# A decode step on one core: the down weights' second load in three parts, the residual on TensorE, one store

## The chip, the core and the metric

The kernel runs on one core of a Trainium2 chip. The core has a matrix engine (TensorE, PE in the profile), three engines for elementwise work (VectorE or DVE, ScalarE or ACT, GpSimd or POOL), an engine that mostly issues transfers (SyncE or SP), and 16 DMA engines that move data between the chip's memory (HBM) and the on-chip memory SBUF. TensorE writes its results to PSUM, a small accumulator memory of 8 banks. The metric is the device time of one execution in microseconds, the median over runs.

## The reference

One decode step of a transformer block: attention over a cache, then a gated feed-forward layer, each behind a layer norm and with a residual. There are 4 sequences (B), one new token each, 512 features (D), 32 heads of 128, a cache of 8192 keys and values per head, and 1792 hidden features (F). All tensors are bf16.

```python
def _A_ref(x, k_cache, v_cache, wq, wo):
    q = (x @ wq).reshape(B, Sq, H, Dh) ...            # per head
    scores = einsum("bhqd,bhkd->bhqk", q, k_cache) * Dh ** -0.5
    o = einsum("bhqk,bhkd->bhqd", softmax(scores), v_cache)
    return o.reshape(B, Sq, H * Dh) @ wo

def _B_ref(x, w_gate, w_up, w_down):
    return (sigmoid(x @ w_gate) * (x @ w_up)) @ w_down

h = x + _A_ref(layernorm(x), k_cache, v_cache, wq, wo)
h2 = h + _B_ref(layernorm(h), w_gate, w_up, w_down)   # the result, 4 x 1 x 512
```

The two caches are 268 MB each, so nearly all of the 551 MB that the kernel reads is cache.

## The kernel before

The program is written out by hand for each engine: `emit` appends an instruction to one engine's list, with tokens of the work it waits for, `prog.dma` does the same for a transfer, and `play` writes the lists out. A token is a semaphore and a value; the 16 DMA engines raise a transfer's semaphore, so one transfer counts 16. Each engine executes its list in order.

**The streaming part.** The 128 pairs of sequence and head are handled as 32 units of 4. For each unit SP loads the keys (8 MB, `k`) and the values (8 MB, `v`) into one of three slots of the SBUF tensor `KV`. VectorE transposes the keys (L334), TensorE computes the scores (L343), ScalarE the exponentials (L368), and TensorE the products with the values (L404). SP's queue holds, in this order: wq, the caches unit by unit, then `wo`, `w_gate`, `w_up` and the down weights. A load is issued when its slot is free; the DMA engines work through the queue in order.

**The tail.** After the last unit's products TensorE projects with `wo` (L474, L479), which leaves h in PSUM (`h_ps`). `layernorm` (L272 to L286) normalises it and writes it transposed. ScalarE copies h to SBUF as `h_sb` in two halves of 256 columns (L485, partitions 0 to 3 and 32 to 35). TensorE computes gate and up (`glu`, L493), ScalarE the sigmoid (L504), VectorE the product and its transposes (L510, L513). The result `hhT` has 14 tiles of 128 hidden features. `down(t)` (L518) multiplies tile t with the down weights: two matmuls, one for each half of the 512 output columns, in different columns of the array, so that the halves lie at PSUM partitions 0 to 3 and 32 to 35 of bank `DN`. VectorE adds `h_sb` (L526) into `o_sb`, SP and ScalarE store a half each (L556), and SP waits for both stores (L558).

**The down weights.** `WDT = (0, 8, 12, 14)` cuts the 14 tiles into three loads, of tiles 0 to 7 (1024 KB), 8 to 11 (512 KB) and 12 and 13 (256 KB), each over all 128 partitions (L554). A tile's matmul waits for its load's token `t_wd`. The second load has one row of 4096 B per partition.

**Filler.** `filler(n)` (L387) issues matmuls whose result nobody reads, in stretches where TensorE waits. Four of them stand ahead of the first `down`.

## Time and profile before

| | |
|---|---|
| median of three runs | 1279.16 us (1279.07 to 1279.24) |
| the profiled execution | 1279.28 us, its span 1278.0 us |
| PE, DVE, ACT busy | 61%, 60%, 5% of the span |
| HBM read | 550.77 MB, 431 GB/s over the span |
| mean granted TensorE clock | 0.814 of full speed |
| the second down load | 512 KB, 32.9 us from issue to landing |

The span runs from the first to the last event of one profiled execution on the core; the execution's own time has 1.28 us more around it. In the profile L518 is line 518 of the kernel before, `KV<-in_B_w_down_dram` a transfer from the down weights into `KV`, SPq and ACTq the issuing of transfers by SP and ScalarE. In a stretch, the DMA share is the busy share of the 16 DMA engines, so a share of 0.06 is one engine at work. The chain of waits is followed back from the last instruction: each piece is what released the next. PEld is TensorE's loading of weights into its array.

### The profile page before, as it was taken

Reading aid. Unit: us, or ns where it says so; the run is one execution under the profiler, and the core shown is the slowest. Engines: PE = TensorE matmul, PEld = TensorE weight load, DVE = VectorE, ACT = ScalarE, POOL = GpSimd, SP = SyncE. Lnnn points to the kernel's source line nnn. Section 1 sums busy time; section 2 is a strip of 40 time slices with the busy share of each in tenths; the row PEclk is TensorE's granted clock in tenths of the full one; section 3 lists DMA queues with packets and bytes.
Section 4 is the critical chain, followed back from the end, with each engine's and each line's share of the span. In section 5 each row is a group of like instructions: output and inputs, shape, how many; then the busy total and the mean of one; then the engine's idle time right before and its main releaser. Section 6 shows DMA issues by size and latency. Waiting matters only on the chain.

```text
span 1278.0 us, 14081 instructions
## 1 busy us (share of the span) xinstructions
PE 782.9 (61%) x4590; PEld 328.4 (26%) x4641; DVE 762.3 (60%) x917; ACT 58.7 (5%) x114; POOL 5.7 (0%) x22
## 2 busy tenths in 40 slices
PE   1676765557755557655567655567555576555577
PEld 0232222223222223222222222222222232222233
DVE  1876665556665557665567655566655566655571
ACT  2000000000000000000000000000000000000001
POOL 1000000000000000000000000000000000000000
PEclk8788877788877788777788777888777888777889
DMA  9999999999999999999999999999999999999998
GB/s 425 429 425 429 427 449 435 427 429 429 453 429 427 429 435 447 429 429 427 445 437 429 429 427 449 433 429 429 427 449 435 427 429 431 449 431 427 429 437 360
DMA packets 10252, 550.83 MB, mean 431 GB/s; under 512 B 1148, under 2 KB 1160, under 8 KB 1416
## 3 DMA queue, kind: packets, MB, share of 16 engines
q1 hardware_dynamic: 10232, 550.77, 99.7%
q8 instruction: 2, 0.03, 0.0%
q14 instruction: 2, 0.02, 0.0%
q10 hardware_dynamic: 16, 0.01, 0.0%
HBM read 550.77 MB, written 0.00 MB: 431 GB/s over the span
## 4 chain that ended last, share of the span: by engine, by line
DMA 60%; PE 20%; DVE 12%; issue 2%; ACT 1%; SPq 0%; DVEq 0%
DMA KV<-in_A_k_cache_dram 58%; PE PS L343 15%; DVE kT L334 12%; PE PS L404 5%; DMA KV<-in_B_w_down_dram 3%; ACT kT L409 1%; PE PS L414 0%; SPq L538 0%; DVE PTz L374 0%; PE PS L518 0%; DVE KV L526 0%; SPq L554 0%; DVEq L112 0%
## 5 line engine op out<-in xcount | busy, mean ns | idle before, releaser
L343 PE MATMUL PS<-kT,Lq 128*128 128x512 bf16 x2048 | 592.0, 422 | 342.6 <-DVE kT L334 325.5
L334 DVE STREAM_TRANSPOSE kT<-KV 128x1024 f32<-128x1024 f32 x512 | 614.2, 1231 | 302.7 <-DMA KV<-in_A_k_cache_dram 237.9
L343 PEld LDWEIGHTS PS<-kT,Lq 128*128 x2048 | 211.0, 103 | 696.4 <-issue 624.2
L374 DVE STREAM_TRANSPOSE PTz<-E_sb 32x512 bf16<-32x512 bf16 x128 | 89.9, 703 | 128.9 <-PE PS L414 125.2
L404 PE MATMUL PS<-KV,PTz 128*16 128x512 bf16 x2048 | 116.9, 381 | 0.0
L378 PE MATMUL PS<-part,headw 128*128 128x2 f32 x64 | 18.8, 363 | 100.5 <-DVE PTz L374 100.5
L368 ACT ACTIVATE E_sb<-PS,negm 128x512 bf16<-128x512 f32 x32 | 22.0, 687 | 1141.7 <-DVE negm L366 1141.7
L404 PEld LDWEIGHTS PS<-KV,PTz 128*16 128x16 bf16 x2048 | 57.7, 109 | 57.3 <-issue 13.6
L414 PE MATMUL PS<-lane,kT 128*128 128x4 f32 x256 | 33.6, 255 | 31.0 <-ACT kT L409 31.0
L361 DVE TENSOR_REDUCE part<-PS 128x1 f32<-128x512 f32 x32 | 22.1, 691 | 38.8 <-PE PS L343 38.8
L414 PEld LDWEIGHTS PS<-lane,kT 128*128 128x128 f32 x256 | 31.0, 191 | 46.3 <-issue 44.9
L378 PEld LDWEIGHTS PS<-part,headw 128*128 128x128 f32 x64 | 16.0, 311 | 103.7 <-DVE PTz L374 103.7
L409 ACT ACTIVATE kT<-PS,rsb 128x512 f32<-128x512 f32 x32 | 22.0, 687 | 64.3 <-PE PS L404 64.3
L387 PE MATMUL PS<-Lq 128*128 128x512 bf16 x33 | 12.1, 425 | 2.7 <-issue 2.0
L453 DVE TENSOR_TENSOR kT<-PS,mask 128x512 bf16<-128x512 f32 x1 | 0.7, 690 | 16.1 <-PE PS L414 16.1
L327 DVE TENSOR_TENSOR Lq<-q_all,mask 128x32 bf16<-128x32 bf16 x32 | 9.7, 302 | 0.0
L387 PEld LDWEIGHTS PS<-Lq 128*128 128x128 bf16 x53 | 5.5, 109 | 8.9 <-issue 5.1
L366 DVE STREAM_TRANSPOSE negm<-mxr 128x32 f32<-128x32 f32 x32 | 6.8, 212 | 1.1
L363 DVE STREAM_TRANSPOSE turn<-part 128x32 f32<-128x32 f32 x32 | 6.8, 212 | 1.1
L395 DVE RECIPROCAL rsb<-PS 128x1 f32<-128x1 f32 x32 | 6.5, 202 | 0.7 <-PE PS L378 0.7
L321 PEld LDWEIGHTS PS<-Lq,headw 128*128 128x128 bf16 x32 | 3.4, 106 | 12.7 <-issue 11.2
L364 DVE TENSOR_SCALAR_CACHE_REDUCE turn<-turn 128x32 f32<-128x32 f32 x32 | 6.0, 186 | 1.1
(67 smaller groups left out, 52.6 us busy)
## 6 DMA issues: line engine op xcount, KB each, us to landing
KV<-in_A_wq_dram SPq DMA_DIRECT2D x1, 4096.0 KB, 12.4
KV<-in_A_wo_dram SPq DMA_DIRECT2D x1, 4096.0 KB, 26.9
KV<-in_B_w_gate_dram SPq DMA_DIRECT2D x1, 1792.0 KB, 31.0
KV<-in_B_w_up_dram SPq DMA_DIRECT2D x1, 1792.0 KB, 34.8
KV<-in_B_w_down_dram SPq DMA_DIRECT2D x1, 1024.0 KB, 32.0
KV<-in_A_k_cache_dram SPq DMA_DIRECT2D x32, 49.7
KV<-in_A_v_cache_dram SPq DMA_DIRECT2D x32, 30.8
KV<-in_B_w_down_dram SPq DMA_DIRECT2D x1, 512.0 KB, 32.9
```

The lines of the kernel that those rows point to most:

```text
L327: t_lq[u] = emit("dve", lambda e, ix: e.tensor_tensor(dst, bass.AP(raw(q_all), at(ix, 0) * (4 * TU) + 4 * (u - TU * t), [[NU * 4, 128], [1 ...
L334: t_tr[u, c] = emit("dve", lambda e: e.transpose(kT[:, (c % 2) * TW:(c % 2 + 1) * TW], KVw[:, o:o + TW]), w, ch="d2p")
L343: ins = e.matmul(bank[SBK], bass.AP(raw(Lq), ix[-1] * 2 + (128 * t + c % 2), [[528, 128], [1, 128]]), rhs, start=False, stop=False, skip_g ...
L361: a = emit("dve", lambda e: e.tensor_reduce(part[:, 0:1], bank[SBK], AX.X, ALU.max), [t_sc[u, NT - 1], t_pool], ch="d2d")
L363: a = emit("dve", lambda e: e.transpose(turn_[:, :], part[:, :]), [a], ch="d2d")
L368: t_exp[u] = emit("act", lambda e: e.activation(E_sb[:, :], bank[SBK], ACT.Exp, bias=negm[:, 0:1], scale=SCALE, accum_out=part[:, 1:2]), [ ...
L374: return [e.transpose(PTz[32 * q:32 * (q + 1), :].rearrange("p (r q c) -> p r q c", r=4, q=4)[:, :, q, :], E_sb[32 * q:32 * (q + 1), :].re ...
L378: t_sum[u] = emit("pe", lambda e: e.matmul(bank[QB[1]][:, 0:2], headw[:, :], part[:, 0:2], start=True, stop=True), [t_ptz[u], t_selc], ch= ...
L387: emit("pe", lambda e: [e.matmul(bank[XS], Lq[:, 0:128], Lq[:, 0:512], start=True, stop=True) for _ in range(n)][-1], [t_ps0, t_lq[NU - 1] ...
L404: made.append(e.matmul(PS[32 * j:32 * j + 16, ob:ob + 512], lhsT, KV[:, slot * SLOT + 512 * k:slot * SLOT + 512 * (k + 1)], start=(k < 4), ...
L409: t_ocp[u] = emit("act", lambda e: e.activation(O_sb, bank[OBK], ACT.Copy, scale=rsb[:, 0:1]), [t_pv[u], t_rs[u]], ch="a2p")
L414: ins = e.matmul(bass.AP(raw(PS), at(ix, 0) * 4 + (512 * EX + 4 * (u - t)), [[4096, 128], [1, 4]]), O_sb[:, 128 * q:128 * (q + 1)], lane[: ...
```

## The change

The second down load (tiles 8 to 11) is issued as three transfers, of partitions 0 to 63, 64 to 115 and 116 to 127, on the same queue and the same semaphore, and its token now counts 48. The residual moves from VectorE's add to TensorE: ScalarE copies h in one instruction to partitions 0 to 3 as `h_sb` (512 columns), and two f32 matmuls with a 4 x 4 identity (`lane[0:B, 0:B]`) write its halves to the two places in bank `DN`, ahead of the first `down` and in the place of the four filler matmuls; all `down` matmuls then add to it. The add becomes two copies from PSUM, VectorE the first half and ScalarE the second, both to partitions 0 to 3 of `o_sb`, and one store from ScalarE's queue takes the place of the two.

```diff
-        h_sb = kT[0:32 + B, TW + 512:TW + 512 + HD]
+        h_sb = kT[0:B, TW + 512:TW + 512 + D]
...
-        o_sb = reg(2, 10240 + 1024, HD)
+        o_sb = reg(2, 10240 + 1024, D)[0:B, :]
...
-        t_wd = [prog.token(f"wd{i}", 16) for i in range(len(WDT) - 1)]
+        WDP = [(0, 128), (0, 64, 116, 128), (0, 128)]
+        t_wd = [prog.token(f"wd{i}", 16 * (len(WDP[i]) - 1)) for i in range(len(WDT) - 1)]
...
-        def f(e):
-            return [e.activation(h_sb[32 * x:32 * x + B, :], h_ps[:, HD * x:HD * (x + 1)], ACT.Copy) for x in range(2)]
-        t_hs = emit("act", f, [t_row], incs=2)
+        t_hs = emit("act", lambda e: e.activation(h_sb, h_ps, ACT.Copy), [t_row])
...
+        def residual(e):
+            return [e.matmul(PS[32 * x:32 * x + B, 512 * DN:512 * DN + HD], lane[0:B, 0:B], h_sb[:, HD * x:HD * (x + 1)],
+                             start=True, stop=False, tile_position=(0, 32 * x), skip_group_check=True) for x in range(2)]
...
-                                 wd_v[:, t, HD * x:HD * (x + 1)], start=(t == 0), stop=(t == NFT - 1),
-                                 tile_position=(0, 32 * x)) for x in range(2)]
+                                 wd_v[:, t, HD * x:HD * (x + 1)], start=False, stop=(t == NFT - 1),
+                                 tile_position=(0, 32 * x), skip_group_check=True) for x in range(2)]
...
-                filler(4)
+                emit("pe", residual, [t_hs], incs=0)
...
-        t_o = emit("dve", lambda e: e.tensor_tensor(
-            o_sb[0:32 + B, :], bank[DN][0:32 + B, 0:HD], h_sb, ALU.add), [t_d, t_hs])
+        t_o = [emit("dve", lambda e: e.tensor_copy(o_sb[:, 0:HD], bank[DN][0:B, 0:HD]), [t_d]),
+               emit("act", lambda e: e.activation(o_sb[:, HD:D], bank[DN][32:32 + B, 0:HD], ACT.Copy), [t_d])]
...
-            prog.dma("sp", f"wd{i}", lambda e, i=i: e.dma_start(
-                wd_v[:, WDT[i]:WDT[i + 1], :], wd_src[:, WDT[i]:WDT[i + 1], :]), [v_done], tok=t_wd[i])
-        t_out = [prog.dma(("sp", "act")[x], f"out{x}", lambda e, x=x: e.dma_start(
-            out.rearrange("b s d -> (b s) d")[:, HD * x:HD * (x + 1)], o_sb[32 * x:32 * x + B, :]), [t_o]) for x in range(2)]
-        emit("sp", lambda e: e.nop(), t_out, incs=0)
+            for a, b in zip(WDP[i], WDP[i][1:]):
+                prog.dma("sp", f"wd{i}", lambda e, i=i, a=a, b=b: e.dma_start(
+                    wd_v[a:b, WDT[i]:WDT[i + 1], :], wd_src[a:b, WDT[i]:WDT[i + 1], :]), [v_done], tok=t_wd[i])
+        t_out = prog.dma("act", "out0", lambda e: e.dma_start(out.rearrange("b s d -> (b s) d"), o_sb), t_o)
+        emit("sp", lambda e: e.nop(), [t_out], incs=0)
```

More of the change, by code (lines that the diff above doesn't have):

```diff
@@ L216, in bass_sequential_preLN__mha_block_cached__glu_gated_glu__decode_kernel @@
         SBK, OBK, EX, XS, XO, QB, DN = 0, 1, 2, 3, 4, (5, 6), 7
-        keys = ["sp", "act", "dve", "pool", "pe", "p2x", "d2x", "x", "pad", "out0", "out1", "wq", "wg", "v0", "v1"]
+        keys = ["sp", "act", "dve", "pool", "pe", "p2x", "d2x", "x", "pad", "out0", "wq", "wg", "v0", "v1"]
         keys += [f"wd{i}" for i in range(len(WDT) - 1)] + [f"wu{i}" for i in range(len(WUC) - 1)] + ["wo"]
```

## The prediction

> **What bounds the kernel now.** I read the page's totals first, then the chain of waits over the last 40 us, then the DMA share in short stretches of the last 2 us, then the order of instructions on each engine around the edit.

> ```profile
> span 1278.0 us, 14081 instructions
> DMA packets 10252, 550.83 MB, mean 431 GB/s; under 512 B 1148, under 2 KB 1160, under 8 KB 1416
> q1 hardware_dynamic: 10232, 550.77, 99.7%
> q10 hardware_dynamic: 16, 0.01, 0.0%
> DMA 60%; PE 20%; DVE 12%; issue 2%; ACT 1%; SPq 0%; DVEq 0%
> ```

> SP's queue (q1) keeps the 16 DMA engines busy for 99.7% of the span. The caches and the weights arrive at 431 GB/s, so one DMA engine moves 431/16 = 26.9 GB/s. Nothing in the change touches the first 1240 us; what can move is the tail. The chain of waits in order of time, from the issue of the first down-weight load:

> ```profile
> 1241.70 0.33 SPq L554
> 1242.02 0.04 issue
> 1242.07 32.92 DMA KV<-in_B_w_down_dram
> 1274.98 0.04 issue
> 1275.03 0.60 PE PS L518 x8
> 1275.63 0.04 issue
> 1275.67 0.43 PE PS L518 x4
> 1276.10 0.02 issue
> 1276.12 0.42 DVE KV L526
> ```

> The three down-weight loads are issued at 1241.7, some 31 us before their bytes move: they wait in the queue behind the last V load and the other weights. The second load lands at 1274.98. The eight matmuls on it end at 1275.63, and then the third load's four start. PE waits for both loads:

> ```profile
> 1241.70 1.28 SPq L554 DMA_DIRECT2D KV<-in_B_w_down_dram  x3
> KV<-in_B_w_down_dram SPq DMA_DIRECT2D x1, 512.0 KB, 32.9
> KV<-in_B_w_down_dram SPq DMA_DIRECT2D x1, 256.0 KB, 33.1
> PEld PS L518 <- DMA KV<-in_B_w_down_dram: 0.7, 2, 0.4
> ```

> Three issues in 1.28 us put the second near 1242.1 and the third near 1242.5, so the third landed at about 1275.6 (1242.5 + 33.1). Both sit on the path. How many DMA engines are still at work by then? The stretches give it: the share times 16 (the last two columns are DMA share and GB/s).

> ```profile
> core 0: us, PE busy (x) PEld busy (x) DVE busy (x) ACT busy (x) POOL busy (x), PEclk, DMA share, GB/s
> 1273.20:1273.60 0.40, 0.00 (x0) 0.00 (x0) 0.36 (x3) 0.00 (x0) 0.00 (x0) 1.00 0.93 358
> 1273.60:1274.00 0.40, 0.13 (x4) 0.14 (x6) 0.37 (x1) 0.00 (x0) 0.00 (x0) 1.00 0.50 190
> 1274.05:1274.25 0.20, 0.20 (x8) 0.16 (x6) 0.00 (x0) 0.00 (x0) 0.00 (x0) 1.00 0.28 113
> 1274.40:1275.00 0.60, 0.51 (x10) 0.18 (x4) 0.00 (x0) 0.00 (x0) 0.00 (x0) 1.00 0.11 44
> 1275.02:1275.20 0.18, 0.17 (x4) 0.15 (x6) 0.00 (x0) 0.00 (x0) 0.00 (x0) 1.00 0.06 23
> ```

> 0.93 is 15 engines, 0.28 four or five, 0.11 two, 0.06 one. So most engines are finished by about 1274.0, four or five run on past 1274.25, two to 1275.0, and one to 1275.2. The last bytes move just before 1275.2 and the third load counts as landed at about 1275.63, some 0.43 us later. The path is set by one or two DMA engines that are over a microsecond behind the rest. One visible source of such lateness is a packet that is not data:

> ```profile
> q1 hardware_dynamic: 59, 0.83, 99.2%
> q8 instruction: 1, 0.02, 3.4%
> ```

> That is 1262 to 1264: one instruction packet of 0.02 MB holds one engine for 3.4% of 16 engines times 2 us, 1.1 us. The queue never runs dry, so that engine stays 1.1 us behind to the end.

> **The change, part by part.** *The second down load in three transfers.* Queue q1 shows how a load's rows are spread. Its 71 loads of 128 rows and one store of 4 rows make 10232 packets: 71 x (128 + 16) + (4 + 4). So a 128-row load is 128 data packets and 16 closing ones, eight rows on each of 16 engines, and a 4-row transfer runs on four engines, one row each. I extend that to the largest number of engines up to 16 that divides the rows: 64 rows are 16 engines x 4, 52 rows 13 x 4, 12 rows 12 x 1. Twelve engines then carry 9 rows instead of 8, one carries 8, and three carry 4. A row is 4096 B, 0.152 us at 26.9 GB/s. The three gain 4 x 0.152 = 0.61 us, the twelve lose 0.15 us. [...]

> What this is worth depends on whether the late two are among those three, which the trace does not name. The ends are a gain of 0.61 us (both are) and a loss of 0.15 us (the latest is among the twelve). I take the gain. [...] With the gain, the latest engine's third load lands at 1275.63 - 0.61 = 1275.02. The other engines were through by 1274.4 and are at most at 1274.4 + 0.15 + 0.43 = 1274.98, so they do not take over. The second load lands at 1274.98 - 0.61 = 1274.37.

> ```profile
> 1270.53 1.69 PE L493 MATMUL PS<-KV,kT 128*4 128x448 bf16 x32 [0.27 <-DVE kT L286]
> 1272.38 0.81 PE L387 MATMUL PS<-Lq 128*128 128x512 bf16 x3 [0.16 <-issue]
> 1273.87 2.18 PE L518 MATMUL PS<-KV 128*4 128x256 bf16 x28 [0.68 <-DMA KV<-in_B_w_down_dram]
> 1266.62 1.02 PE L479 MATMUL PS<-kT,lane 128*4 128x512 f32 x2 [0.78 <-ACT kT L478]
> 1270.32 0.75 ACT L485 ACTIVATE kT<-PS 4x256 f32<-4x256 f32 x2
> ```

> PE can use the gain. Eight matmuls take 0.60 us and four 0.43, so one more adds 0.0425, and all 28 take 0.43 + 24 x 0.0425 = 1.45 us from their start at 1273.87 to 1275.32. They still wait for the third load and end at 1275.06 + 0.43 = 1275.49 instead of 1276.10: -0.61 us. SP issues two more transfers, 0.43 us each at most (three took 1.28 us); they stand behind 31 us of queued bytes, so they cost nothing, and SP's next duty, the store's end, is 33 us away. Without that backlog they would cost 0.86 us.

> *The residual on PE.* Two f32 matmuls of 256 columns take the place of four filler matmuls. One f32 matmul of 512 columns (L479) shows as two records and 1.02 us, so the two cost about the same together, 1.0 us, from 1272.2 to 1273.2, in a gap that lasts until 1273.87. Their input, the copy of h on ScalarE, was ready at 1271.07 and now is one instruction of 512 columns instead of two of 256. Cost 0; the cover is 0.65 us of waiting for the first down load, and without it the cost would be about 0.2 us, 1.0 less the filler's 0.81. PE's granted clock is 1.00 in all rows above.

> *The add becomes two half copies, the two stores one.*

> ```profile
> 1276.12 0.42 DVE L526 TENSOR_TENSOR KV<-PS,kT 36x256 bf16<-36x256 f32 x1 [2.15 <-PE PS L518]
> 1276.56 0.35 SPq L556 DMA_DIRECT2D out_dram<-KV  x1
> 1276.57 0.28 ACTq L556 DMA_DIRECT2D out_dram<-KV  x1
> L465 DVE CAST kT<-PS x1: 291/291/291, 1263.4 to 1263.4; 128x128 bf16<-128x128 f32 x1
> L286 DVE CAST kT<-PS 128x16 bf16<-128x16 f32 x1 | 0.2, 175 | 0.4 <-PE PS L282 0.4
> 1263.93 1.90 PE L474 MATMUL PS<-KV,kT 128*4 128x512 bf16 x32
> 1265.97 0.60 ACT L478 ACTIVATE kT<-PS 128x512 f32<-128x512 f32 x1 [3.26 <-PE PS L474]
> SPq L558 <- DMA out_dram<-KV: 1.1, 1, 1.1
> ```

> VectorE's copies grow from 175 ns at 16 columns to 291 at 128, 1.04 ns a column, so 256 take 0.42 us: no change. ScalarE's half takes 0.37 (0.75 for two in L485) but starts later after PE: 0.14 us in L478 (1263.93 + 1.90 to 1265.97), against 0.02 for VectorE in the chain. It ends 0.14 + 0.37 = 0.51 us after PE where VectorE ends 0.44 after: +0.07. The store's issue stands behind ScalarE's copy in its own queue and also waits for VectorE, and SP's final wait hangs on it. Against that, SP's store issue of 0.35 us, the one that ended last (1276.91), gives way to ScalarE's 0.28 (1276.85): -0.06. The rows of 1 KB instead of 512 B add under 0.04 us at 26.9 GB/s. Together 0, between -0.15 and +0.15.

> Sum: -0.61 us. The profiled execution took 1279.28 us (span 1278.0 and 1.28 around it), which gives 1278.67; the median of the runs, 1279.16, gives 1278.55. I predict **1278.6**.

> **The rivals.** *(a) The latest engine is not relieved.* For it: three of sixteen are relieved, and the trace has no engine numbers. [...] The loads land as now, or 0.15 later: 1279.16 to 1279.31, say 1279.2.

> *(b) Rows of neighbouring partitions get in each other's way, and it turns slower.* Each load of before spreads its rows over all 128 partitions at once; the three new ones fill 64, 52 and 12 neighbouring ones. If two engines that write the first two, and four that write the last, halve and quarter each other's rate, an ordinary engine needs 4 x 0.152 x 2 + 4 x 0.152 x 2 + 0.152 x 4 = 3.04 us for its nine rows, against 1.22 now. That is +1.82 us on engines that finish about 1274.0, so the last bytes move at about 1275.8 instead of 1275.2: +0.6, to 1279.8. It decides once the nine rows cost these engines over 1.2 us more than now. For it: 0.93 of 16 engines busy shows no slack to absorb a slower rate. Against: the engines are not in step, the shares fall over more than 1 us, so fewer meet; then it only eats the gain. [...]

> *(c) The end costs more than it gives*: ScalarE's copy and its own wait add 0.15 us and the stretch before it goes as forecast: 1278.8. With (a) it is 1279.4.

> *(d) The code of the tail moves an instruction packet onto another engine or moment*, up to 1.1 us either way: 1278.0 to 1280.2.

> **How the numbers follow.** The forecast has 0.42, (a) 0.25, (b) 0.18, (c) 0.09, (d) 0.06. The forecast's own range is 1278.4 to 1278.8 (its ±0.15, and 0.1 for the spread of runs, 1279.07 to 1279.24). To leave out no more than 2 in 10 the range must reach through (a) to the price of (b): 1278.2 to 1279.8. A change of 0.2%, 2.6 us, is about what a measurement of this kernel can tell from none. No case except several at once reaches it: the part of the run that the change can touch is the last 5 us. Faster 0.01, within 0.96, slower 0.03.

> **What would show it.** Right: q1 has 10249 packets (70 x 144, 64 + 16, 52 + 13, 12 + 12), q10 still 16; the chain has the second load landing near 1274.4 and the third near 1275.0, with the two engines' stretch of 1274.40 to 1275.00 gone; PE's last matmul ends near 1275.5. Rival (a): these stay at 1274.98 to 1275.13 and 1275.6 to 1275.8. Rival (b): the DMA share between 1273.2 and 1274.0 stays near 1 for longer while GB/s falls, and many engines finish late. Rival (c): ScalarE's copy ends over 0.15 us after VectorE's. The residual is wrong if the first down matmul starts after 1273.87. The prediction fails altogether if the loads of the caches run at another rate than 431 GB/s, which nothing in the change gives cause for.

## The result: slower by 2.35 us, and the profile after

The changed kernel takes 1281.63 us (median of 19 runs, 1281.40 to 1282.37) against 1279.28 (19 runs, 1279.07 to 1279.49): 2.35 us more, a ratio of 1.0019 with a 95% interval of 1.0012 to 1.0025. The difference of 0.19% is just within the 0.2% that was called no change, though the interval reaches past it; the time lies outside the range of 1278.2 to 1279.8, on the side away from the forecast of 1278.6. Rival (b) was the one that pointed this way, and its price of 1279.8 was too small.

The page of the changed kernel, and its chain of waits in order of time (start, duration, what), answer to those of before:

```profile
span 1280.3 us, 14084 instructions
q1 hardware_dynamic: 10249, 550.77, 99.6%
q10 hardware_dynamic: 16, 0.01, 0.0%
```

```profile
1241.71 33.76 DMA KV<-in_B_w_down_dram
1275.46 0.14 issue
1275.60 2.96 PE PS L521 x28
1278.56 0.02 issue
1278.59 0.41 DVE KV L529
```

The packets are split as forecast: 10249 on SP's queue. But the chain has another shape. TensorE now waits for the *first* down load, which nobody had touched: it lands at 1275.46, where before it landed at 1273.74. From there TensorE works through all 28 matmuls without a stop, in 2.96 us instead of the 1.45 worked out from before. The busy time of the engines in stretches of one microsecond (the last three columns are granted TensorE clock, DMA share, GB/s), first before and then after:

```profile
1272.00:1273.00 1.00, 0.84 (x11) 0.31 (x4) 0.55 (x2) 0.13 (x1) 0.00 (x0) 1.00 1.05 424
1273.00:1274.00 1.00, 0.32 (x5) 0.14 (x6) 0.94 (x3) 0.00 (x0) 0.00 (x0) 1.00 0.75 289
1274.00:1275.00 1.00, 0.91 (x16) 0.52 (x12) 0.00 (x0) 0.00 (x0) 0.00 (x0) 1.00 0.16 61
1275.00:1276.00 1.00, 0.93 (x12) 0.36 (x12) 0.00 (x0) 0.00 (x0) 0.00 (x0) 1.00 0.01 4
```

```profile
1272.00:1273.00 1.00, 0.92 (x16) 0.09 (x4) 0.39 (x1) 0.31 (x1) 0.00 (x0) 1.00 1.07 164
1273.00:1274.00 1.00, 0.00 (x0) 0.00 (x0) 0.95 (x3) 0.00 (x0) 0.00 (x0) 1.00 0.90 195
1274.00:1275.00 1.00, 0.00 (x0) 0.00 (x0) 0.15 (x1) 0.00 (x0) 0.00 (x0) 1.00 0.96 193
1275.00:1276.00 1.00, 0.40 (x8) 0.33 (x10) 0.00 (x0) 0.00 (x0) 0.00 (x0) 0.93 0.39 113
1276.00:1277.00 1.00, 1.00 (x12) 0.52 (x8) 0.00 (x0) 0.00 (x0) 0.00 (x0) 0.50 0.17 66
```

Two things are new. From 1272 to 1273 the DMA engines are all busy in both kernels, but move 164 GB/s instead of 424, and in the changed kernel they stay busy at under 200 GB/s until 1275, when before most had long finished. And TensorE's granted clock, 1.00 in all of the last stretch before, falls to 0.50 at 1275.87, so that nearly all of the down matmuls run at half the clock.

The end itself became shorter. Before, VectorE ended at 1276.12 + 0.42 = 1276.54 and the span 1.46 us later; now it ends at 1279.00, and the span 1.3 us later, so the new end gains about 0.15 us.

The times at which the three down loads landed are used below for all runs. They are of one profiled execution of each kernel: the last of the 16, 43 and 16 arrivals on each load's semaphore in the trace, in us from the span's start (the 43 are of three transfers on 16, 13 and 12 engines with two raised at issue; other splits have other counts). The last column is read from the same traces' records of single DMA packets: a packet of 8192 B is one row of the first down load, which every kernel here issues in the same way, and the column has the median duration in ns of those that start after 1272.

```text
                     1st load  2nd load  3rd load   PE ends   GB/s 1273 to 1274   8192 B row
before                1273.74   1274.99   1275.63   1276.10   289                 314
changed kernel        1275.46   1276.96   1277.48   1278.56   195                 759
whole_load            1273.90   1275.15   1275.78   1276.25   291                 314
split_only            1275.23   1276.81   1277.42   1278.10   219                 584
filler_kept           1275.99   1277.22   1277.83   1278.30   221                 648
three_columns         1273.76   1275.08   1275.71   1276.63   292                 314
halves                1276.08   1277.37   1278.00   1279.41   184                 816
halves_src            1276.11   1277.60   1278.24   1279.43   158                 826
halves_dst            1273.70   1274.95   1275.58   1276.05   266                 314
halves_stride         1273.59   1274.83   1275.46   1275.93   250                 314
quarters              1275.83   1276.98   1277.61   1279.16   193                 691
spread_64_52_12       1274.43   1275.79   1276.43   1277.32   186                 483
relief_10             1274.50   1275.72   1276.35   1277.25   193                 388
```

So the third load is 1.85 us later, and the rows of the untouched first load take 759 ns instead of 314 while the split load moves beside them. TensorE ended 0.47 us after it before (1276.10 - 1275.63) and ends 1.08 after it now: 0.61 more. With 0.15 less at the end that makes 1.85 + 0.61 - 0.15 = 2.31 us, the 2.3 by which the span grew. The experiments had to show which part of the change causes the late loads and which the slow matmuls.

### The profile page after: what moved, and what is told of

It is laid out like the page before. It is cut to its first block, busy times and chain, and to the rows that moved or that the text cites. A ratio compares the mean times of both kernels' runs of the same rounds, so it can differ in the third digit from the quotient of the medians.

```text
span 1280.3 us, 14084 instructions
## 1 busy us (share of the span) xinstructions
PE 780.5 (61%) x4591; PEld 328.4 (26%) x4641; DVE 762.9 (60%) x917; ACT 59.0 (5%) x114; POOL 5.7 (0%) x22
## 2 busy tenths in 40 slices
DMA packets 10269, 550.83 MB, mean 430 GB/s; under 512 B 1169, under 2 KB 1177, under 8 KB 1433
## 3 DMA queue, kind: packets, MB, share of 16 engines
q1 hardware_dynamic: 10249, 550.77, 99.6%
HBM read 550.77 MB, written 0.00 MB: 430 GB/s over the span
## 4 chain that ended last, share of the span: by engine, by line
DMA 34%; PE 11%; DVE 7%; issue 1%; another core or an unknown queue 1%; ACT 0%; SPq 0%; DVEq 0%
DMA KV<-in_A_k_cache_dram 31%; PE PS L344 8%; DVE kT L335 7%; DMA KV<-in_B_w_down_dram 3%; PE PS L405 3%; ACT kT L410 0%; PE PS L415 0%; PE PS L521 0%; SPq L541 0%; DVE PTz L375 0%; DVE KV L529 0%; DVEq L112 0%
## 6 DMA issues: line engine op xcount, KB each, us to landing
KV<-in_A_wo_dram SPq DMA_DIRECT2D x1, 4096.0 KB, 26.9
KV<-in_B_w_down_dram SPq DMA_DIRECT2D x2, 256.0 KB, 33.8
```

## The experiments

The theory at this point (N): transfers of few neighbouring partitions make DMA engines write into the same part of SBUF and slow one another; the late loads then leave TensorE idle, and its clock falls. Its rivals: the missing filler alone (F), the mere number of transfers (T), the uneven rows, or neighbouring addresses in HBM (H).

### One part at a time

**whole_load**, the changed kernel without its split:

```diff
-        WDP = [(0, 128), (0, 64, 116, 128), (0, 128)]
+        WDP = [(0, 128), (0, 128), (0, 128)]
```

> The changed kernel with the second down load in one transfer of 128 partitions again; residual, half copies and single store as changed. Theory N (the rows of 64, 52 and 12 neighbouring partitions slow one another): the third load lands near 1275.6 again, the granted clock in the down stage is 1.00, and only the store's end is left of the change: about 0.15 us faster than before, 1279.1. Theory F (the missing filler is what costs, by a lower TensorE clock): the 28 matmuls still take over 2 us from the first one to the end and the time is 0.5 us or more above before, 1279.8 or later.

Measured: 1279.10 us against 1279.26, ratio 1.0000 (0.9990 to 1.0010). Its chain is that of before:

```profile
1241.89 33.26 DMA KV<-in_B_w_down_dram
1275.15 0.04 issue
1275.20 0.60 PE PS L521 x8
1275.80 0.03 issue
1275.83 0.43 PE PS L521 x4
1276.25 0.02 issue
1276.28 0.41 DVE KV L529
```

The residual, the half copies and the store together cost nothing that shows. The forecast of 0.15 us less fits the medians, but the interval is wider than that. Without filler the clock is 1.00 here, so the filler's removal alone is not what lowers it.

**split_only**, the kernel before with the split alone (`WDP` and the loop over it, as in the change):

> The kernel before with the three transfers alone; filler, add and two stores as before. Theory N: the third load lands 1.85 us later than before, near 1277.5, as in the changed kernel; the end comes 1.85 us later if the clock holds (1281.1), and about 2.45 us later if the wait of 2.3 us behind the filler lowers the clock all the same (1281.7). Theory F: the clock holds because the filler is there, and the loads are late only by the extra row, 0.15 us: 1279.4.

Measured: 1281.55 us, ratio 1.0019 (1.0009 to 1.0028): the whole loss, from the split alone. The first load is late here too. The groups of down matmuls in order of time, with the idle time before each in brackets:

```profile
1272.15 0.81 PE L388 MATMUL PS<-Lq 128*128 128x512 bf16 x3 [0.16 <-issue]
1275.37 1.04 PE L519 MATMUL PS<-KV 128*4 128x256 bf16 x16 [2.40 <-DMA KV<-in_B_w_down_dram]
1276.86 1.20 PE L519 MATMUL PS<-KV 128*4 128x256 bf16 x12 [0.45 <-DMA KV<-in_B_w_down_dram]
```

```profile
1276.00:1278.10 2.10, 1.60 (x20) 0.45 (x14) 0.00 (x0) 0.00 (x0) 0.00 (x0) 0.80 0.06 23
```

In this execution the clock fell only during the last group (its mean is 0.80 in the stretch just above, third number from the end), and TensorE ended 0.68 us after the third load. The runs spread from 1280.91 to 1282.33. So four filler matmuls did not hold the clock here either, with a wait of 2.4 us behind them.

**filler_kept**, the changed kernel with TensorE kept busy:

```diff
                 emit("pe", residual, [t_hs], incs=0)
+                filler(11)
```

> The changed kernel with eleven filler matmuls (2.4 us) between the residual and the first down matmul. If TensorE's halved clock costs 0.6 us of the result and comes from its idle time of 2.7 us, the granted clock stays 1.00 through the down stage, the loads land as in the changed kernel (third near 1277.5), PE ends about 0.45 us after that instead of 1.1, and the time is 0.6 us below the changed kernel, 1281.0. If the clock is lowered by something else, the time is 1281.6 as before.

Measured: 1281.01 us, 0.62 below the changed kernel's 1281.63, as expected, with nine of its ten runs below the lowest of the changed kernel's nineteen; ratio to before 1.0013 (1.0003 to 1.0022). The down matmuls' groups (mean duration in ns behind the busy time), in the changed kernel and here:

```profile
L521 PE MATMUL PS<-KV 128*4 128x256 bf16 x28 | 2.9, 393 | 2.7 <-DMA KV<-in_B_w_down_dram 2.7
```

```profile
L521 PE MATMUL PS<-KV 128*4 128x256 bf16 x28 | 2.0, 272 | 0.8 <-DMA KV<-in_B_w_down_dram 0.7
```

The stretch of filler_kept's down matmuls, with the clock third from the end:

```profile
1275.90:1278.40 2.50, 2.02 (x28) 1.01 (x28) 0.08 (x1) 0.08 (x1) 0.00 (x0) 1.00 0.08 30
```

The clock holds at 1.00 although the loads are as late as ever. The 0.61 us is the clock's: with the wait filled it did not fall, and TensorE ended 0.47 us after the third load (1278.30 - 1277.83), as before. The changed kernel's clock was low from 1275.87 to 1279.28, 3.41 us, and every complete stretch of one clock in its trace is a multiple of that. Behind TensorE's idle time it fell after 2.7 us in the changed kernel, 2.4 in split_only, 1.7 and 1.8 in spread_64_52_12 and relief_10 below, and not after 1.1 us in whole_load. How much of the down stage ran at the low clock differs between these executions: all from 1275.87 on in the changed kernel, a part of the last group in split_only.

### What about the split slows the loads

**three_columns**, three transfers that each cover all partitions. `WDP` is `(0, 1, 2, 3)` for this load, so that `a` counts its transfers:

```diff
...
+                lo, hi = (WDT[i], WDT[i + 1]) if i != 1 else ((8, 10), (10, 11), (11, 12))[a]
+                prog.dma("sp", f"wd{i}", lambda e, lo=lo, hi=hi: e.dma_start(
+                    wd_v[:, lo:hi, :], wd_src[:, lo:hi, :]), [v_done], tok=t_wd[i])
```

> The changed kernel with the second down load in three transfers that each cover all 128 partitions (2, 1 and 1 of its 4 tiles: rows of 2048, 1024 and 1024 B). Theory T (three transfers with their own closing packets and issues cost the time, or smaller rows): the third load lands 1 us or more later than before. Theory N: it lands within 0.3 us of 1275.6, and the time is that of the one-transfer variant, 1279.1 to 1279.4.

Measured: 1279.12 us, ratio 1.0000 (0.9990 to 1.0009); the third load at 1275.71. Three transfers, more packets and smaller rows cost nothing that shows. Theory T falls. TensorE ended late in the profiled execution, but not because of the loads: the clock was 0.50 from 1264 to 1270.

```profile
1264.00:1270.00 6.00, 5.23 (x26) 1.03 (x19) 1.05 (x4) 1.13 (x3) 0.00 (x0) 0.50 1.00 423
```

It fell there at 1263.42, though no idle time of TensorE in the 11 us before was over 0.9 us. So the length of a single idle time does not decide alone; what else does stays open.

**halves**, equal rows for all engines:

```diff
-        WDP = [(0, 128), (0, 64, 116, 128), (0, 128)]
+        WDP = [(0, 128), (0, 64, 128), (0, 128)]
```

> The changed kernel with the second down load in two transfers, partitions 0 to 63 and 64 to 127: every engine has 4 + 4 rows, none has a ninth. Theory N: still late, the third load at 1276.8 or later, the time 1280.7 to 1281.6. If the uneven 9, 8 and 4 rows were the cause: as with one transfer, 1279.1.

Measured: 1282.24 us, ratio 1.0023 (1.0014 to 1.0033), above the 1281.6 expected at most and no faster than the changed kernel; the third load lands at 1278.00. The uneven rows are not the cause. The other three of this set change only which partitions and which rows of HBM each half takes (`a` is 0 or 64; `TO` and `FROM` stand for the slices written below). halves_src and halves_dst leave the second load's weights in the wrong partitions and are there for the time alone:

```diff
...
+                to, fr = (slice(a, b), slice(a, b)) if i != 1 else (TO, FROM)
+                prog.dma("sp", f"wd{i}", lambda e, i=i, to=to, fr=fr: e.dma_start(
+                    wd_v[to, WDT[i]:WDT[i + 1], :], wd_src[fr, WDT[i]:WDT[i + 1], :]), [v_done], tok=t_wd[i])
...
# halves_stride: TO and FROM are slice(a // 64, 128, 2)
# halves_src:    TO is slice(a, b), FROM is slice(a // 64, 128, 2)
# halves_dst:    TO is slice(a // 64, 128, 2), FROM is slice(a, b)
```

> As the two halves, but the even partitions in one transfer and the odd ones in the other, in SBUF and in HBM alike. Same count of transfers, engines and rows per engine. Theory N: each half now reaches all parts of SBUF, so most of the delay goes: the third load within 0.6 us of 1275.6, the time below 1280. If halving the partitions as such costs (fewer rows per transfer, a different division over the engines): as the contiguous halves.

> The halves of 64 neighbouring partitions in SBUF, but the rows read from HBM are every second one (so the second load's weights stand in the wrong rows: the output is not the reference's). Theory S (the clash is on SBUF's side): as slow as the contiguous halves. Theory H (the clash is neighbouring addresses in HBM): as fast as the strided halves.

> The converse: every second partition in SBUF, 64 neighbouring rows of HBM per transfer (the second load's weights stand in the wrong rows: the output is not the reference's). Theory S: as fast as the strided halves. Theory H: as slow as the contiguous halves.

Measured: halves_stride 1279.01 us, ratio 0.9999 (0.9989 to 1.0008); halves_src 1281.54, 1.0018 (1.0008 to 1.0028); halves_dst 1279.05, 0.9998 (0.9989 to 1.0008). The stretch from 1273 to 1274 of halves, halves_src, halves_dst and halves_stride, in this order:

```profile
1273.00:1274.00 1.00, 0.00 (x0) 0.00 (x0) 0.96 (x3) 0.00 (x0) 0.00 (x0) 1.00 1.01 184
```

```profile
1273.00:1274.00 1.00, 0.20 (x2) 0.00 (x0) 0.95 (x3) 0.00 (x0) 0.00 (x0) 1.00 0.87 158
```

```profile
1273.00:1274.00 1.00, 0.16 (x4) 0.17 (x6) 0.90 (x3) 0.00 (x0) 0.00 (x0) 1.00 0.69 266
```

```profile
1273.00:1274.00 1.00, 0.38 (x8) 0.27 (x8) 0.93 (x4) 0.00 (x0) 0.00 (x0) 1.00 0.65 250
```

Among these four the destination alone settles it. With 64 neighbouring partitions of SBUF as destination the loads move 184 and 158 GB/s in this stretch, fed by either set of HBM rows; with every second partition the third load lands at 1275.46 and 1275.58, where with one load it landed at 1275.63, again with either set. In the fast two the share falls because engines are done, and the first load's rows still take 314 ns; in the slow two the engines are busy at a fraction of their rate, and these rows take 816 and 826 ns. Theory H falls.

**quarters**, four transfers of 32 partitions (`(0, 32, 64, 96, 128)` in the same place), to see whether the count of neighbouring partitions is what sets the delay:

> The changed kernel with the second load in four transfers of 32 neighbouring partitions, two rows per engine each. [...] If it is the count of partitions, the delay of the halves (2.4 us) doubles, third load near 1280.

Measured: 1281.76 us, ratio 1.0019 (1.0009 to 1.0029), third load at 1277.61: no worse than halves, and nowhere near the 1280 of a doubled delay. So the count of partitions is not what sets the rate: from 1273 to 1274 the quarters move 193 GB/s and the halves 184.

### Which DMA engines are late

**spread_64_52_12** and **relief_10** were meant to test the relief of late engines without the clash:

```diff
...
# spread_64_52_12: 64 even, 52 odd, 12 odd partitions: 9, 8 and 4 rows per engine
+                rows = slice(0, 128) if i != 1 else (slice(0, 128, 2), slice(1, 105, 2), slice(105, 128, 2))[a]
# relief_10: 64 even, 60 odd, 4 odd partitions: 9, 8 and 4 rows per engine too
+                rows = slice(0, 128) if i != 1 else (slice(0, 128, 2), slice(1, 121, 2), slice(121, 128, 2))[a]
```

> The changed kernel's three transfers of 64, 52 and 12 rows, so 9, 8 and 4 rows per engine, but over every second partition (the even ones; 52 odd ones; the last 12 odd ones), which took the clash away in the halves. If the late engines are the three with 4 rows, the third load lands 0.6 us earlier than before, near 1275.0, and the time is near 1278.5. Rival (a), the late engines are among the others: it lands between 1275.5 and 1275.8 and the time is 1279.0 to 1279.3.

> As before it, but 64 even, 60 odd and 4 odd partitions: by the same division engines 0 to 9 carry 10 or 11 rows and engines 10 to 15 four. The eleven tiny loads let me read the two latest engines as numbers 10 to 12. If so, the second load ends on an engine that was not the latest: the third lands near 1275.1 and the time is 1278.5 to 1278.7, below both kernels. If the late ones are below 10, it lands 0.3 us or more later than before, 1279.4 or more.

Measured: 1280.48 us, ratio 1.0010 (1.0000 to 1.0020), and 1280.36, 1.0009 (1.0000 to 1.0019). Neither expectation held: the third load came 0.80 and 0.72 us later than before. relief_10 could not have shown the relief that was expected of it: 60 rows run on 15 engines, not on 10, and the numbers that the expectations give the engines are an assumption that no trace shows. The semaphore of its second load has 37 arrivals, 16 + 15 + 4 and two raised at issue, so by the division four engines carry nine rows, eleven carry eight and one carries four. The stretches from 1272 on show what both have in common, in spread_64_52_12 and then relief_10:

```profile
1272.00:1273.00 1.00, 0.85 (x12) 0.09 (x4) 0.45 (x2) 0.23 (x1) 0.00 (x0) 1.00 1.09 313
1273.00:1274.00 1.00, 0.00 (x0) 0.00 (x0) 0.97 (x3) 0.00 (x0) 0.00 (x0) 1.00 0.80 186
1276.00:1277.00 1.00, 1.00 (x12) 0.48 (x8) 0.00 (x0) 0.00 (x0) 0.00 (x0) 0.50 0.00 0
```

```profile
1272.00:1273.00 1.00, 0.84 (x12) 0.09 (x4) 0.45 (x2) 0.23 (x1) 0.00 (x0) 1.00 1.10 311
1273.00:1274.00 1.00, 0.00 (x0) 0.00 (x0) 0.96 (x3) 0.00 (x0) 0.00 (x0) 1.00 0.93 193
```

Part of the clash is back (186 and 193 GB/s), although every transfer takes every second partition. Equal halves of 64 avoid it; 64, 52 and 12 rows or 64, 60 and 4 do not. In relief_10 a row of 4096 B takes 159 to 169 ns until 1272.25, when 53 of the 128 have started, and 273 to 361 from 1272.50 to 1272.75, so its first transfer, of 64 rows, is mostly through before the clash begins. Which rows each engine gets, and why these clash, no run shows, so the two runs say nothing sure about the relief. The clock also fell in both at about 1275.8, and TensorE ended 0.89 and 0.90 us after the third load instead of 0.47.

**probe** and **probe_late** asked directly. They are the kernel before with tiny loads of k rows at the end of the queue. Such a load runs on k engines (the load of 10 rows has 10 arrivals and one raised at issue), and, as the arrivals below bear out, it lands some 0.18 us after the last of its engines is through with the third down load:

```diff
...
+        t_pr = [prog.dma("sp", f"pr{k}", lambda e, k=k, n=n: e.dma_start(
+            reg(2, 20000 + 32 * n, 32)[0:k, :], B_w_down[0:k, 0:32]), [v_done]) for n, k in enumerate(PK)]
...
# PK, probe: 1, 2, 4, 6, 8, 10, 12, 13, 14, 15, 16; probe_late: 10, 11, 12, 13, 16
```

> The kernel before with eleven tiny loads (64 B a row) at the end of SP's queue, of 1, 2, 4, 6, 8, 10, 12, 13, 14, 15 and 16 rows, each with its own semaphore; their data is not used. If a load of k rows runs on the k lowest-numbered engines, one lands when the latest of those engines is through with the third down load. Theory of the prediction (the two late engines are among 13 to 15): loads of up to 12 or 13 rows land near 1274.9, those of 15 or 16 near 1275.7 or later. Rival (a) (the late engines are among the first twelve): loads of 12 rows or fewer already land as late as the one of 16. The time is up to 1 us longer than before by the extra packets.

> The kernel before with five tiny loads (64 B a row) of 10, 11, 12, 13 and 16 rows at the end of SP's queue, and GpSimd writing one unused column behind each. Each tiny load adds about 0.17 us to the one before it on the same engines. If the latest engines are numbers 10 to 12, the step between two of the loads of 10, 11 and 12 rows is 0.4 us or more, and those of 13 and 16 rows add only about 0.17 each. If they are among 13 to 15, the large step comes after 12.

Measured: 1279.11 and 1278.97 us in one run each, so the tiny loads cost nothing that shows. Neither shows the large step that I had expected: each tiny load adds about 0.18 us on the engines that it uses, which hides it. GpSimd's writes behind the loads of 10, 11, 12, 13 and 16 rows in probe_late come in even steps:

```profile
1275.27 0.10 POOL L560 MEMSET pdum<- 128x1 f32 x1 [1267.80 <-DMA KV<-in_B_w_down_dram]
1275.45 0.10 POOL L561 MEMSET pdum<- 128x1 f32 x1
1275.64 0.10 POOL L562 MEMSET pdum<- 128x1 f32 x1
1275.82 0.10 POOL L563 MEMSET pdum<- 128x1 f32 x1
1276.00 0.10 POOL L564 MEMSET pdum<- 128x1 f32 x1
```

The single arrivals on the semaphores of that run tell more (the latest ones of each load, us):

```text
third down load   1274.639   1275.037   1275.381   1275.394
10 rows           1274.827   1275.219
11 rows           1275.019   1275.407
12 rows           1275.211   1275.593   and 1275.571
13 rows           1275.401   1275.775   and 1275.748   and 1275.535
16 rows           1275.588   1275.955   and 1275.925   and 1275.689
```

Two of the four late engines (1274.639 and 1275.037) are already in the load of 10 rows and come back 0.18 to 0.19 us later in each next one. The load of 10 rows landed before the third down load did, so the two latest are not among its engines. The load of 12 rows brings a new arrival at 1275.571, that of 13 rows one at 1275.535, each 0.15 to 0.19 after one of the two latest, and that of 16 rows brings none. So the two latest sit on the engines that the loads of 12 and of 13 rows add: in the change's split one of them has nine rows and the other eight, and neither has four. The first probe reads the same way (new arrivals at 1275.652 with 12 rows and 1275.664 with 13). That rests on larger loads using the same engines as smaller ones and more, which the returning arrivals bear out, and on two executions of the kernel before. That the late engines are the same two in the changed kernel is not shown, but its landings fit: four rows less on the latest engine would bring its third load some 1.28 us after its first (1.89 - 0.61, by the table), and it came 2.02 us after it there, 2.19 in split_only and 1.84 in filler_kept.

## Why the prediction was wrong

*What bounds the kernel*: right. The tail is set by the landing of the down loads, and nothing before it moved (the instruction packet of rival (d) starts at 1262.25, before at 1262.29).

*Split of rows*: right in the counts (10249 packets; arrivals of 16 + 13 + 12). *Relief of the late engines*: wrong. The step that failed first is "I take the gain": that the two late engines are among the three relieved was assumed without a row, and by the probes both are outside them; two more late ones are among the ten that the load of 10 rows uses. So no run shows the gain of 0.61 us that the forecast is made of; the third load came 1.85 us later instead. By itself the missing gain would have been rival (a), 1279.2.

*Rates of the split transfers*: the step that cost the time. The working priced every row at 0.152 us wherever it lands, and left the clash to rival (b) at 0.18. The packet records say what a row cost: those of 4096 B that start from 1272 to 1273 take 0.160 us in the kernel before (median) and 0.434 in the changed kernel. (b)'s mechanism, that rows of neighbouring partitions get in each other's way, is shown by halves_src and halves_dst (third load at 1278.24 against 1275.58). The halving and quartering in its sum were assumed, and no run shows them; the rows took 2.7 times as long (0.434 / 0.160). Its price for ordinary engines was not far off: the twelfth of sixteen third-load arrivals moved from 1274.47 to 1276.07, +1.60 us, where (b) had +1.82. What (b) missed is that late engines suffer too. I held against it that engines out of step do not meet. They do: when the ordinary engines start on the split second load, the late ones still write the *first* (the split load's first rows land at 1273.36, the first load's last at 1275.46). Of that load's arrivals the eleventh moved by 0.22 us, the last four by 1.21 to 1.73, and it carried the rest with it. That they meet in the same parts of SBUF fits the destination's part in it, but no trace shows where an engine writes. So (b)'s "last bytes 0.6 us later" was 1.85.

*The residual on PE at cost 0*: right in itself. It took 0.60 us from 1272.32, not 1.0, and whole_load is no slower than before. *The filler*: here the prediction said that PE's granted clock is 1.00 in all rows and went on as if it would stay so. No rival named the clock. Its fall cost 0.61 us, as a consequence of the late loads: the forecast gave a price for the cover's end (0.2 us) without asking what the clock would do in a longer wait, which became 2.7 us.

*The end*: 0 with bounds of 0.15 each way; the span's end gave about -0.15, at the lower bound. ScalarE's copy did not start late: it began at 1278.59, with VectorE's, and took 0.375 us. The 0.14 us of delay taken from the row of L478 did not carry over.

*Chances*: 0.18 for the direction that came was low: the trace of before had no load to a part of the partitions, so nothing spoke for 0.152 us a row in the split transfers, and the gain rested on a premise without a row.

## What to carry to other kernels

If a load has to be split, the splits that cost nothing that shows here were those over columns (three_columns, ratio 1.0000) and into the even and the odd partitions (halves_stride, 0.9999); unequal sets of every second partition clashed again (186 and 193 GB/s from 1273 to 1274). A load split into groups of neighbouring partitions moved under half the rate here (164 GB/s from 1272 to 1273, instead of 424) and dragged down the loads beside it, the one ahead included. A late DMA engine can only be relieved if it is known which one it is; tiny loads of growing row counts at the end of the queue gave a reading of it here at no cost that showed. A filler's worth is not its own cover: it shows when the wait behind it grows (whole_load, without filler, idled for 1.1 us and lost nothing that shows; eleven filler matmuls in the changed kernel's wait of 2.7 us gained 0.62), so price the wait together with TensorE's clock.

No variant clearly beats the kernel before. whole_load, three_columns, halves_stride and halves_dst have medians 0.1 to 0.3 us below it, all with intervals around 1; halves_dst is not a kernel to use, since its weights stand in the wrong partitions.

## What was not expected of the hardware

And the late engines are not late from the start. In the trace of the kernel before, the last of a cache load's 16 arrivals comes 0.62 us after the first for the load that lands at 51.9 us, 1.12 for the one at 71.8 and 1.69 for the one at 91.7; instruction packets of 0.31 and 0.93 us stand in between, at 63.1 and 87.4 us. From there it shrinks slowly, to 1.49 us at 1233.4. After the packet of 1.10 us at 1262.3 the last but one arrival, too, comes 1.48 us after the first, where it came 0.85 after it just before. So the lateness looks like what these packets leave behind in a queue that never runs dry; the trace does not name the engines, so that is argued and not shown.
